# Seven block products in every token tile but the first, shared products copied between PSUM banks, and one written order for everything behind the first tile

## The chip, the cores and the metric

The kernel runs on one core of a Trainium2 chip. The engines are PE (TensorE: matmuls, with weight loads listed apart as PEld), DVE (VectorE), ACT (ScalarE), POOL (GpSimd) and SP (SyncE, here used to issue transfers). The metric is the device time of one execution in microseconds (us). Three runs of the kernel before gave 226.59, 226.91 and 228.11 us; the median is 226.91.

## The reference

Attention over pooled keys and values feeds a maxout layer. In short:

```python
k_p = k.reshape(B, H, Sp, 8, D).mean(axis=3)          # B, H, S, D = 8, 8, 576, 64; Sp = 72
v_p = v.reshape(B, H, Sp, 8, D).mean(axis=3)
attn = softmax(q @ k_p.T / sqrt(D))
x = (attn @ v_p).transpose(0, 2, 1, 3).reshape(4608, 512)
h = maximum(maximum(x @ w1, x @ w2), x @ w3)          # 768 wide
out = h @ w_out                                       # 4608 x 512, float32
```

Inputs are float32 and are cast to 16 bits on their way into SBUF (the keys of batch 0 excepted).

## The kernel before

**Tiles.** The 4608 tokens are nine tiles of 512, tile n = 0 to 8; attention comes in eight batches of 576 tokens, so that tile n holds the end of batch n-1 and the beginning of batch n. `xT` is a ring that holds the attention output transposed, `hT` the hidden layer transposed.

**Maxout as a linear part and two relu inputs.** The kernel uses h = x w1 + max(0, x (w2 - w1), x (w3 - w1)). The linear part times w_out is one matrix `wm` (`linear`, L344), so the output is x wm + max(...) w_out. A plain tile needs 6 row blocks x 2 weights x 4 matmuls of 512 columns for the hidden layer (`hidden_part`, L357), and 4 x (4 + 6) matmuls for the output (`project`, L400).

**Seven products.** A 2 x 2 block matrix product can be made from seven block products and some sums in place of eight (Winograd's form). `PRODUCTS` names the operands of the seven: S1 to S4 are sums of weight blocks (`fold_w`, `fold_out`), T1 to T4 sums of data blocks. Products 1, 6, 5 and 3 are accumulated one after the other in one PSUM bank, A, whose running value is read out after each; product 2 has bank B; 7 and 4 share bank C. Each hidden product is four matmuls of 256 columns (L789), each output product ten (L713). Before the change the hidden layer is made so in tiles 6, 7 and 8 (`seven`, L753), the output in tiles 2, 3, 4, 7 and 8 (`out_seven`, L643). There the value of product 1 is copied by ACT to SBUF (L795) and added to product 2 by DVE (L766); the top rows of `hT` then come from one more ACT copy (L799) and a DVE maximum of two SBUF operands (L769).

**Attention of a batch.** Keys and values are pooled by sums of eight rows. `fold_steps` (L157) does it in three sums, on POOL for most batches (L161, L162, L164). `pool_v` (L177) pools V of batch 0 by matmuls. Keys are transposed on PE (`keys`, L196) and copied into zero-padded tiles `kz` (`turn_k`, L204). Queries are transposed on PE in batches 0 to 2 (`turn_q`) and by a DMA from SP in the others (`T`, L302). Scores go to PSUM and ACT takes exp of them (L223): eight steps of 576 columns (`scores`), or, in batch 7, nine of 512 (`scores_flat`). `values` (L264) multiplies by the pooled V; DVE divides by the row sums (L274, L276). The result is transposed on PE (batches 0 to 2, L259) or by DMA from SP (L253).

**Order.** The program is written by hand: every engine and every DMA queue runs its instructions in program order, and waits where data or a buffer is not there. `block(0, ...)` runs tile 0 with steps of batches 0 and 1 between its parts; `MIDDLE` does so for tiles 1 to 4; `block(5, LEAD, ...)` for the hidden part of tile 5; `ORDER` and `weave` for the last three tiles. In these lists `k`, `K`, `q`, `Q`, `s`, `v`, `x` and `T` are attention steps, `1a` to `7c` hidden products, `o1` to `o7` output products. `held` and `gate` make POOL's fold wait for a certain DVE sum.

**PSUM** has eight banks. In the middle of the kernel before, scores have four (two pairs), the FFN three, transposes one. In its last part `SC` has two, `PA` two, `BC` one, `PO` one, and `val` two.

**Loads.** Inputs are loaded through POOL's DMA queue, two buffers for each of k, q and v, and outputs are stored mostly through SP's.

## Time and profile before

| what | value |
|---|---|
| median of three runs | 226.91 us (226.59 to 228.11) |
| the profiled execution | 228.01 us |
| its span, first to last instruction | 226.3 us |
| granted TensorE clock | 1.000 |
| busy: PE / DVE / ACT / POOL | 214.7 / 148.6 / 122.3 / 138.6 us |
| read from HBM / written | 34.60 / 9.44 MB |

The profiled execution is one of its own, with its time beside its span; durations of single instructions come from it, and it is 1.1 us above the median. "Busy" counts an instruction from start to end; matmuls overlap, so the mean of one matmul is longer than its share of a dense row, and the chain of waits shows that share better. A row of a group names the source line, the engine, the operation, output and inputs with their shapes, how often it ran, the busy time and the mean of one.

### The profile page before, as it was taken

Reading aid. Unit: us, or ns where it says so; the run is one execution under the profiler, and the core shown is the slowest. Engines: PE = TensorE matmul, PEld = TensorE weight load, DVE = VectorE, ACT = ScalarE, POOL = GpSimd, SP = SyncE. Lnnn points to the kernel's source line nnn. Section 1 sums busy time; section 2 is a strip of 40 time slices with the busy share of each in tenths; the row PEclk is TensorE's granted clock in tenths of the full one; section 3 lists DMA queues with packets and bytes.
Section 4 is the critical chain, followed back from the end, with each engine's and each line's share of the span. In section 5 each row is a group of like instructions: output and inputs, shape, how many; then the busy total and the mean of one; then the engine's idle time right before and its main releaser. Section 6 shows DMA issues by size and latency. Waiting matters only on the chain.

```text
span 226.3 us, 4691 instructions
## 1 busy us (share of the span) xinstructions
PE 214.7 (95%) x1807; PEld 146.4 (65%) x1807; DVE 148.6 (66%) x292; ACT 122.3 (54%) x221; POOL 138.6 (61%) x111
## 2 busy tenths in 40 slices
PE   6788999999999999999999999699999999999993
PEld 2467745558656555965686568355677677788882
DVE  3668876038595385876679668535668886898840
ACT  2267524755874577238624862475687446555330
POOL 7974300999949967787677758999500913872020
PEclk9999999999999999999999999999999999999999
DMA  6999999989759999659999599965241534200265
GB/s 167 210 197 197 208 207 208 203 163 224 128 106 191 217 220 208 112 129 151 199 226 191 31 216 236 182 126 132 58 107 29 122 61 95 46 3 0 55 203 164
DMA packets 47351, 33.54 MB, mean 148 GB/s; under 512 B 27041, under 2 KB 42337, under 8 KB 47329
## 3 DMA queue, kind: packets, MB, share of 16 engines
q0 software_dynamic: 16944, 16.98, 48.1%
q1 hardware_dynamic: 29936, 15.87, 33.0%
q10 hardware_dynamic: 448, 0.39, 0.7%
q8 instruction: 14, 0.23, 0.5%
q14 instruction: 9, 0.07, 0.1%
HBM read 34.60 MB, written 9.44 MB: 195 GB/s over the span
## 4 chain that ended last, share of the span: by engine, by line
PE 69%; DMA 15%; POOL 11%; issue 1%; DVE 1%; ACT 1%; POOLq 0%
PE pw L362 21%; PE oA L713 9%; DMA vt<-in_v_dram 8%; PE pA L789 7%; PE po L416 7%; PE po L412 5%; PE oC L713 4%; PE psc L218 4%; DMA mw<-in_moe_w_dram 4%; PE pC L789 3%; POOL half L161 3%; DMA xT<-xn 3%; PE pav L268 3%; PE oB L713 2%; POOL half L162 2%; PE pB L789 2%
## 5 line engine op out<-in xcount | busy, mean ns | idle before, releaser
L362 PE MATMUL pw<-xT,mw 128*128 128x512 f16 (+1 forms) x336 | 72.8, 348 | 1.9 <-DMA xT<-xn 1.6
L362 PEld LDWEIGHTS <-mw 128*128 128x128 f16 x336 | 31.6, 98 | 22.3 <-DMA xT<-xn 1.8
L370 DVE TENSOR_TENSOR hT<-t,pw 128x512 f16<-128x512 f16 (+1 forms) x42 | 25.4, 609 | 25.1 <-ACT et L223 17.8
L223 ACT ACTIVATE et<-psc 72x576 f16<-72x576 f32 (+2 forms) x54 | 35.2, 661 | 6.8 <-PE psc L218 6.7
L161 POOL TENSOR_TENSOR half<-vt 72x2048 f32<-72x2048 f16 x7 | 28.4, 4061 | 13.8 <-DMA vt<-in_v_dram 13.3
L162 POOL TENSOR_TENSOR half<-half 72x1024 f32<-72x1024 f32 (+1 forms) x13 | 27.3, 2098 | 11.0 <-DVE rcp L274 6.1
L368 ACT ACTIVATE t<-pw 128x512 f16<-128x512 f32 (+1 forms) x42 | 22.5, 537 | 16.2 <-PE pw L362 15.8
L276 DVE TENSOR_TENSOR xn<-pav,rcp 128x512 f16<-128x512 f32 x40 | 27.7, 692 | 1.4
L416 PE MATMUL po<-mwo,hT 128*128 128x512 f16 (+1 forms) x102 | 23.5, 366 | 0.0
L218 PE MATMUL psc<-qT,kz 128*128 128x320 bf16 (+2 forms) x120 | 22.4, 278 | 0.8 <-DVE qT L194 0.6
L218 PEld LDWEIGHTS <-kz 128*128 128x128 bf16 x143 | 13.1, 98 | 13.3 <-ACT qT L194 1.1
L161 POOL TENSOR_TENSOR half<-ktFalse 96x1536 f32<-96x1536 f16 x6 | 18.7, 3125 | 4.0 <-issue 2.9
L564 POOL TENSOR_TENSOR pad<-xT 128x256 f16<-128x256 f16 x8 | 5.9, 732 | 22.5 <-ACT pad L795 13.9
L795 ACT CAST pad<-pA 128x512 f16<-128x512 f32 x27 | 15.6, 588 | 7.2 <-PE pA L789 7.0
L268 PEld LDWEIGHTS <-et 72*128 72x128 f16 x320 | 15.1, 98 | 3.6 <-issue 0.4
L723 ACT COPY osb<-oA 128x512 f32<-128x512 f32 x12 | 7.0, 586 | 19.2 <-PE oA L713 19.2
L274 DVE RECIPROCAL rcp<-pav 128x8 f32<-128x8 f32 x40 | 8.2, 204 | 14.0 <-PE pav L268 13.6
L412 PE MATMUL po<-wm,xT 128*128 128x512 f16 (+1 forms) x68 | 16.6, 366 | 0.0
L268 PE MATMUL pav<-vp,et 72*128 72x65 f16 x320 | 16.4, 194 | 0.1
L421 ACT COPY osb<-po 128x512 f32<-128x512 f32 (+1 forms) x16 | 9.2, 573 | 12.0 <-PE po L416 12.0
L789 PEld LDWEIGHTS <-sw 128*128 128x128 f16 x144 | 13.7, 98 | 2.5
L766 DVE TENSOR_TENSOR pad<-pad,pC 128x512 f16<-128x512 f16 x18 | 12.3, 685 | 3.9 <-PE pC L789 3.6
(122 smaller groups left out, 380.0 us busy)
## 6 DMA issues: line engine op xcount, KB each, us to landing
out_dram<-osb SPq DMA_DIRECT2D x38, 128.0 KB, 5.5
ktFalse<-in_k_dram POOLq DMA_DIRECT2D x7, 576.0 KB, 8.2
qb<-in_q_dram POOLq DMA_DIRECT2D x7, 576.0 KB, 13.0
vt<-in_v_dram POOLq DMA_DIRECT2D x7, 576.0 KB, 17.5
mw<-in_moe_w_dram POOLq DMA_DIRECT2D x9, 256.0 KB, 9.4
out_dram<-osb SPq DMA_DIRECT2D x8, 256.0 KB, 7.4
ktTrue<-in_k_dram SPq DMA_DIRECT2D x3, 384.0 KB, 5.2
out_dram<-ob SPq DMA_DIRECT2D x8, 128.0 KB, 2.6
```

What stands on the lines that cost most here:

```text
L161: yield e.tensor_tensor(out=f, in0=t[:, :, 0:4, :], in1=t[:, :, 4:8, :], op=ALU.add)
L162: yield e.tensor_tensor(out=f[:, :, 0:2, :], in0=f[:, :, 0:2, :], in1=f[:, :, 2:4, :], op=ALU.add)
L218: nc.tensor.matmul(out, kz_all[b % 2][f % 2][rows, h, :], qTs[b][rows, n + i0:n + i1, 64 * (h % 2):64 * (h % 2) + 64], start=True, stop=True)
L223: nc.scalar.activation(out=out, in_=in_, func=FT.Exp, scale=1.0 / 64.0)
L268: nc.tensor.matmul(pav[:, h // 4, 65 * (h % 4):65 * (h % 4) + 65], ets[b][:, h, c0:c0 + 128], vp_all[:, b, h, :], start=True, stop=True)
L276: nc.vector.tensor_tensor(out=xn, in0=pv[:, :, :, 0:D], in1=rcp.to_broadcast([128, 2, 4, D]), op=ALU.mult)
L362: mm = nc.tensor.matmul(pw, w_sb[wi][:, kc, bass.ts(jc, 128)], x[:, kc], start=(kc == 0), stop=(kc == KCH - 1))
L370: nc.vector.tensor_tensor(out=hT[:, jc, c0:c1], in0=t, in1=pw, op=ALU.max)
L412: nc.tensor.matmul(po, tokens(128 * m, 128 * m + 128)[:, kc], wm_sb[:, kc, c], start=(kc == 0), stop=False)
L416: nc.tensor.matmul(po, hT[:, jc, bass.ts(mm, 128)], wo_sb[:, jc, c], start=False, stop=(jc == JCH - 1))
L713: nc.tensor.matmul(p, left, right, stop=(r == 4), skip_group_check=True, start=(i in FIRST and r == 0 and (m == 0 or n == LAST)))
L789: mm = nc.tensor.matmul(p[:, w], a[:, kc, bass.ts(g, 128)], b[:, kc, :], start=(i in FIRST and w + kc == 0), stop=(w + kc == 2), skip_grou ...
```

## The change

Behind the hidden layer of tile 0 there is one written order, `ORDER`, of some 500 steps, in place of `MIDDLE`, `LEAD`, `ORDER` and `weave`.

- The hidden layer and the output of tiles 1 to 8 are all made from seven products; only tile 0 stays plain.
- Product 1 is copied by ACT from bank A into bank B (PSUM to PSUM), and product 2 accumulates there. For the hidden layer the top rows of `hT` then come straight from banks B and A: a relu of one half by ACT, a maximum with the other half by DVE, each for 256 columns. For the output one ACT copy takes bank B out. A first matmul into the bank, `zB`, comes before.
- V of batch 1 is pooled on PE like that of batch 0. The folds on POOL are cut into pieces (`pieces`): five for K, six for V; the third sum of K is made on PE by accumulating two transposes, that of V on DVE. Each piece waits for the DVE sum of SBUF operands that stands last ahead of it (`shared`).
- All four key copies are ACT's. All scores of batches 1 to 7 are flat (nine steps of 512).
- The sums of output weights for the w_out rows (`G`) are POOL's; the data sums `t` and `u` are DVE's.
- Behind tile 0 PSUM holds `SC` 2, `PA` 2, `PB` 1, `PC` 1 and `val` 2 banks.
- The pooled V is kept for three batches in place of eight.

In the order, `p` is half a row block of tile 0's output, `<k4` a load, `K4` and `V4` pieces of folds, `P` V of batch 1 on PE, `t1` to `t4` and `u1` to `u4` data sums, `S`, `f`, `F`, `G` weight sums, `1d` to `7d` output products. Cut to its core:

```diff
     def load_v(b, eng, dtype=F16, cuts=(0, H)):
-        if b == 0:
+        if b < 2:
...
     def new_kp(b):
-        kps[b] = sb2.tile([96, 6, D], BF16, name="kp", tag="kp")
+        kps[b] = sb2.tile([96, 2, 6, D], F16, name="kp", tag="kp")
...
     def keys(b, tag):
...
         for i in range(3):
-            nc.tensor.transpose(pkt[:, i, :],
-                                kps[b][:, 2 * i:2 * i + 2, :].rearrange("p i d -> p (i d)"),
-                                ident[0:96, 0:96])
+            for j in range(2):
+                nc.tensor.matmul(pkt[:, i, :], kps[b][:, j, 2 * i:2 * i + 2, :].rearrange("p i d -> p (i d)"),
+                                 identh[0:96, 0:96], start=(j == 0), stop=(j == 1))
...
-        for par, evac in enumerate((nc.vector.tensor_copy, nc.scalar.copy)):
+        for par in range(2):
             for odd in range(2):
-                (evac if b > 2 else nc.vector.tensor_copy)(
+                nc.scalar.copy(
...
+    def both(out, a, b, op, e=nc.vector):
+        t = e.tensor_tensor(out=out, in0=a, in1=b, op=op)
+        if e is nc.vector:
+            shared[:] = [t]
+        elif shared[0] is not None:
+            after([t], shared[0])
...
+    def hidden_product(n, i, g):
...
+        p = bank(of(i), n, g)
+        za, zb = PRODUCTS[i]
+        for w in range(2):
...
+            for kc in range(2):
+                mm = nc.tensor.matmul(p[:, w], a[:, kc, bass.ts(g, 128)], b[:, kc],
+                                      start=(i in (1, 7) and w + kc == 0),
+                                      stop=(w + kc == 2), skip_group_check=True)
...
+        if i == 1:
+            nc.scalar.copy(out=bank("B", n, g), in_=p)
+        elif i in (6, 5):
+            nc.scalar.copy(out=y[:, i == 5], in_=p)
+        elif i in (2, 3):
+            t0 = sb2.tile([128, HALF], F16, name="t0", tag="t0")
+            nc.scalar.activation(out=t0, in_=p[:, 0], func=FT.Relu)
+            nc.vector.tensor_tensor(out=h_of(g)[:, i - 2], in0=t0, in1=p[:, 1], op=ALU.max)
+        if i in (5, 7) and (n, 12 - i, g) in done:
+            plus(1)
+        if i == 4:
+            plus(0)
+            shared[:] = [nc.vector.scalar_tensor_tensor(
+                out=h_of(g + JH), in0=y[:, :, 0], scalar=0.0, in1=y[:, :, 1],
+                op0=ALU.max, op1=ALU.max)]
...
+    def out_product(n, i):
...
+        if i == 1:
+            nc.scalar.copy(out=bank("B", n, "d"), in_=p)
+        elif i != 4 and i != 7:
+            nc.scalar.copy(out=o(int(i in (5, 3)))[:, :, lo if i in (2, 3) else hi], in_=p)
...
+    def pieces(what, b):
...
+        e = nc.gpsimd
+        for i in range(0, n, 2):
+            c = slice(i, i + 2)
+            yield e.tensor_tensor(out=f[:, c], in0=t[:, c, 0:4, :], in1=t[:, c, 4:8, :],
+                                  op=ALU.add)
+        for i in range(0, n, n // 2):
+            c = slice(i, i + n // 2)
+            yield e.tensor_tensor(out=two[:, c], in0=f[:, c, 0:2, :], in1=f[:, c, 2:4, :],
+                                  op=ALU.add)
+        if what == "v":
+            both(vp_all[:, b % 3, :, 0:D], two[:, :, 0, :], two[:, :, 1, :], ALU.add)
             yield
...
+    def piece(what, b):
         if (what, b) not in folding:
+            folding[what, b] = pieces(what, b)
+        gate = shared[0]
+        op = next(folding[what, b])
+        if op is not None and gate is not None:
+            after([op], gate)
...
+              16: [(None, "f f")], 17: [(1, "K")], 20: [(None, "F F")],
+              22: [(None, "F F G G G G")]}, (hidden,))
+    first_tiles = project(0)
...
+    nc.tensor.matmul(psum([128, NB], F32, name="zB", tag=PB[0], bufs=PB[1]),
+                     warm[:, 0:128], warm, start=True, stop=True)
...
+        S S q10 <k3 q11 p q12 k1 p P1 K2 K2 s10 p S q13 K2 K2 P0 s11 S s12 K2 s13 s14 V2 s15
+        s16 V2 s17 V2 s18 p q20 v10 q21 p q22 k2 v11 V2 p V2 V2 x10 v12 <v3 <q3 x11 K3 p K3
+        s20 K3 v13 K3 s21 1a x12 K3 x13 t1 t3 t2 p V2 s22 <k4 t4 V3 2a q23 v14 6a V3 1b s23
+        s24 7a V3 5a s25 V3 2b V3 s26 3a s27 4a s28 6b T3 V3 <q4 <v4 1c x14 v20 5b 2c 6c K4
+        K4 v21 x20 <k5 3b k3 K4 7b 5c x21 v22 1a 4b 3c K4 K4 x22 7c 2a s30 t1 u1 t2 s31 1d
...
+        7b 2d 1c 6d 6c 4b 5c 7c u4 5d 4c 3c 2c 7d 3d 4d
...
+    last = out_last(LAST)
+    for i in range(4):
+        sum_h(LAST, i)
     for i, m in ((1, 0), (1, 1), (2, 0), (2, 1), (6, 0), (6, 1), (7, 0), (5, 0), (5, 1),
                  (7, 1), (3, 0), (3, 1), (4, 0), (4, 1)):
-        outs(i, m)
-    for _ in tiles:
-        pass
+        last(i, m)
```

## The prediction

> **What bounds the kernel now.** The page's busy row comes first, then the table of 10 us stretches.

> ```profile
> PE 214.7 (95%) x1807; PEld 146.4 (65%) x1807; DVE 148.6 (66%) x292; ACT 122.3 (54%) x221; POOL 138.6 (61%) x111
> ...
> 140.00:150.00 10.00, 7.85 (x61) 4.77 (x58) 4.92 (x10) 5.13 (x10) 9.77 (x4) 1.00 0.99 153
> ...
> 160.00:170.00 10.00, 10.00 (x98) 7.31 (x96) 6.39 (x14) 8.60 (x17) 1.30 (x2) 1.00 0.41 87
> ...
> 190.00:200.00 10.00, 10.00 (x84) 7.96 (x83) 8.87 (x14) 6.05 (x12) 7.54 (x11) 1.00 0.23 52
> ```

> The columns of a stretch are its length, PE, PEld, DVE, ACT, POOL, granted clock, DMA share, GB/s. PE is the bound almost everywhere: it loses 4.9 us in the first 30 us, about 2 us at 140 to 150, and what follows its last matmul at 222.5. With ACT at 8.6 of 10, or DVE at 8.9 and POOL at 7.5, PE stays full. So PE work is the currency, and the question is what the other engines do when PE has less.

> **The price of PE work.** In the chain in order of time each piece ends where the next dense one starts:

> ```profile
> 68.90 0.86 PE po L412 x4
> 70.33 1.29 PE po L416 x6
> ...
> 104.39 0.86 PE pw L362 x4
> ...
> 161.33 0.44 PE pA L789 x4
> ...
> 199.79 1.09 PE oA L713 x10
> ```

> Four 512-wide matmuls take 0.864 us, a block product of four 256-wide ones 0.437, an output product of ten 1.09. A token tile therefore costs: hidden plain 12 groups x 0.864 = 10.37, hidden by seven 21 x 0.437 = 9.18; output plain 4 x (0.86 + 1.29) = 8.62, output by seven 7 x 1.09 = 7.63.

> - Removed: tiles 1 to 5 change hidden form, 5 x 1.19 = 5.9 us; tiles 1, 5 and 6 change output form, 3 x 0.99 = 3.0. Together 8.9.
> - Added: batch 1's V is pooled on PE, 12 matmuls 256 wide, 1.3; the key transposes become six matmuls in place of three (three step by 0.14 in the timeline), 7 x 0.14 = 1.0; the matmul into PB, 0.2. Together 2.5. Flat scores cost nothing: 9 x 0.217 per batch, where eight pairs took 1.95.
> - Net on PE: **-6.4 us**.

> The check is to add up the same prices from 37.2 us on (the first output product, at 37.94, less 0.7 for batch 1's turns, which move behind it). Before: 8.6 + 51.8 + 27.5 + 25.9 + 38.1 for matrix products, 13.7 scores, 9.3 values, 5.2 turns, in all 180.1. PE ended 185.3 us later, so **5.2 us were stalls**, 2.2 of them the transposed DMA at 145. After: the order adds up to 165.9, zB 0.2, the last tile's output 7.6, in all 173.7. The tail may cost 0.5 more: it ends with DVE additions and 128 KB stores (2.6 us to land) in place of a half copy and 64 KB (2.1). So the time hangs on the new stalls S: change = -6.4 + 0.5 + (S - 5.2).

> **ACT.** Its rows are 0.59 us for 512 columns, but back to back they start closer:

> ```profile
> 194.56 0.59 ACT L421 COPY osb<-po 128x512 f32<-128x512 f32 x1 [1.09 <-PE po L416]
> 195.04 0.59 ACT L795 CAST pad<-pA 128x512 f16<-128x512 f32 x1
> ```

> The pitch is 0.48; for exp 0.49, for a 256-wide relu 0.28 (0.39 less the same 0.11), for one key copy 0.485. The change gives ACT the copies that DVE made of the keys (four now, 1.94 per batch), one more exp per batch, and five evictions per row block. The copy from PSUM to PSUM has no row. Its ends are the 256-wide copy (0.37) and the key copy's cost per column taken to 512 (0.85); I take the 0.59 copy of equal shape. Along the order, ACT asks 10.9, 10.4 and 10.4 us in the first three stretches of 10 us of PE work, then 8.5 to 9.1, then less. From 5.8 to 26.1 us it asks 3.6 more than PE. PE can't run ahead of that: scores have two banks, eight of batch 1's stand with no other matmul between them (8 x 0.49 against 8 x 0.22), and a block product often follows the copy of its own bank by only 0.1 to 0.5 us. I charge **3.0 us**. At the full 0.59 row the excess would be 10.3.

> **POOL and loads, early.** The rows that the pieces are cut from:

> ```profile
> 39.40 4.06 POOL L161 TENSOR_TENSOR half<-vt 72x2048 f32<-72x2048 f16 x1 [13.33 <-DMA vt<-in_v_dram]
> 43.54 2.34 POOL L162 TENSOR_TENSOR half<-half 72x1024 f32<-72x1024 f32 x1
> ...
> 49.36 3.11 POOL L161 TENSOR_TENSOR half<-ktFalse 96x1536 f32<-96x1536 f16 x1
> 52.54 1.81 POOL L162 TENSOR_TENSOR half<-half 96x768 f32<-96x768 f32 x1
> ```

> A fold of K is 3 x 1.04 + 2 x 0.9 = 4.9 us, of V 4 x 1.02 + 2 x 1.17 = 6.4. The third steps leave POOL (1.0 and 1.3): K's goes to PE, V's to DVE (0.42 to 0.69 by its 512-wide f16 rows; I take 0.42). The four wo sums (G) on POOL have no row of 768 columns; three times the undisturbed 0.67 of a 256-wide one gives 2.0 as an upper end, 1.5 by the V row's rate is the lower. At some 1.9 each, behind DVE's sums at about 36, they end at 44, and K of batch 2 lands at 45.1 as before. Its fold ends near 50.7 with the load of K3 queued ahead, while PE would ask for it at 37.4 + 10.8 + 1.2 = 49.4. That 1.3 us wait lets ACT catch up, so it isn't added. Then V's six pieces end at 57; only behind them does POOL issue V3 and Q3. Two loads at POOL's queue rate of 0.2 MB/us (2.07 MB from 20 to 30 us; a load is 0.59) put Q3 down near 65; its transpose took 4.0 to 10.2 us (median 7.0); scores of batch 3 stand at 37.4 + 30.2 + 3 = 70.6. I charge **1.0**.

> **DVE.** Its pitch is 0.60 for a 512-wide PSUM sum, 0.335 and 0.47 for the f16 sums. The order asks 124.9 us against 165.9 of PE; the densest stretch, 67.0 to 75.4, asks 2.3 too much once. With ACT's near misses later I put **2.2** on the rest of the order; before, stalls apart from the one wait were 3.0. So S = 3.0 + 1.0 + 2.2 = 6.2 and the change is -6.4 + 0.5 + 1.0 = -4.9. The profiled execution took 228.0 (span 226.3, and 1.7 around it), 1.1 above the median; the same difference on the median gives **222.0 us**.

> **Rivals.** *POOL holds DVE up.* A DVE sum of two SBUF operands that meets a running POOL sum was long here:

> ```profile
> L597 DVE TENSOR_TENSOR so<-wm x2: 417/882/1348, 62.3 to 64.0; 128x512 f16<-128x512 f16 x2
> L597 DVE TENSOR_TENSOR so<-so,wm x1: 424/424/424, 63.7 to 63.7; 128x512 f16<-128x512 f16 x1
> ```

> At 62.3 POOL ran the last V step, and the same sum took 1.35 in place of 0.42. While POOL folds (10 to 107 us of the order) DVE has some 63 such sums: t, u, the maxima, V's last step. It works 77 us of these 97, so 20 are free, or 0.32 per sum. At the mean excess of 0.46 the sums cost 29: 9 too much, and the result is about **231 us, slower**. This decides from 0.32 us on. For it: DVE and POOL both run at 70 to 95% there, and POOL is up to 7.6 us behind PE. Against it: a piece is at most 1.2 us (4.06 before), starts only when the last such DVE sum written ahead of it has ended, and at 190 to 200 both engines were busy and PE full. [...]

> *The loads come late.* V3, Q4 and V4 are issued behind POOL's pieces, and a piece that waits for its load holds the next issue.

> ```profile
> busy tenths in 40 slices 2051100611500710061025003307000000000000
> DMA to landing us min/median/max: 8.0/14.3/23.4
> ```

> These are V's landings. With 8 us after the issue, V4 is folded at 89 and DVE wants it at 37.4 + 49.5 + 4 = 91: free. At 11 it is 3 late, after two such steps 6; at 14.3 it is 10. Since K and Q went ahead of V in the 14.3 (6 us of queue), I hold 8 to 11 likelier. At 3 to 4 us more than my sum the result is **225.5, no change**.

> *Nothing new stalls.* S of 1 to 2 gives **217**; before's stretch from 150 to 220 shows that woven products can be full.

> *The change doesn't do what it says*: if the copied product had to be copied back or added by DVE, 0.6 us x 31 would come to DVE; the diff has no such step, and I give it nothing of its own.

> **How the numbers follow.** The measurement tells 1% apart (224.6 to 229.2). Forecast, 219 to 224.6: 0.48. Nothing stalls: 0.17. Loads late: 0.19. POOL holds DVE: 0.13, and 0.03 for a slower end by something else. So faster 0.65, same 0.19, slower 0.16. The range reaches from 216.5, below S = 1, to 229.5, where the late loads and a light form of the collisions end; left out are the collisions' full price and ACT's 10.3.

> **What would show it.** Right: PE's busy time near 208, ACT's share above 60%, PE holes between 42 and 72 us with ACT's exp or a POOL fold as what was waited for, none after 150. Wrong: DVE sums t, u and the maxima with means well above 0.42, 0.55 and 0.69; DVE's V step waiting for POOL; POOL waiting for V's landing in every batch; block products of 0.437 that lie 0.2 or more apart all through the order.

## The result, and the profile after

The changed kernel takes 251.96 us (median of 4 runs, 250.88 to 255.90) where the kernel before, on the same chip, takes 226.75 (226.53 to 228.11): a ratio of 1.108, 95% interval 1.1015 to 1.1147. It is 25 us slower, and the forecast was 5 us faster, with a range that ended at 229.5. The profiled execution took 250.88 us, with a span of 249.1 and a mean granted clock of 0.966; the one of before had 1.000. Where the runs of a kernel below fall into two groups, both are given: the three longer ones that were profiled have holes behind transposes that land late, but no shorter run of the same kernel was profiled beside them, so that these holes make the whole difference isn't shown.

The busy row and the clock row of the page of the changed kernel (the clock row has 40 slices of 6.2 us, each digit the granted clock in tenths):

```profile
PE 220.0 (88%) x2119; PEld 177.4 (71%) x2119; DVE 185.7 (75%) x347; ACT 152.6 (61%) x306; POOL 113.4 (46%) x118
...
PEclk9999999999799999976999799799999999999999
```

And the table by stretches of 10 us, with the columns as before (length, PE, PEld, DVE, ACT, POOL, clock, DMA share, GB/s):

```profile
60.00:70.00 10.00, 6.92 (x59) 5.58 (x58) 7.73 (x10) 6.08 (x14) 9.99 (x10) 0.83 1.04 174
100.00:110.00 10.00, 4.54 (x45) 3.96 (x43) 2.93 (x7) 3.62 (x8) 0.65 (x1) 0.96 1.26 169
130.00:140.00 10.00, 8.10 (x65) 6.42 (x64) 9.18 (x14) 5.42 (x12) 8.87 (x9) 0.83 1.00 170
150.00:160.00 10.00, 7.90 (x67) 6.44 (x65) 6.04 (x12) 3.71 (x8) 7.26 (x8) 0.85 1.23 227
200.00:210.00 10.00, 10.00 (x110) 8.94 (x108) 9.73 (x22) 6.80 (x14) 0.00 (x0) 1.00 0.38 84
```

Two things are to be seen. Between 60 and 160 us PE has holes in several stretches, and in the deepest of them or just behind, the clock is below 1; between them lie full stretches at full clock (10.00 of 10 from 140 to 150). Behind 170 us, with POOL idle, PE is as full as it was before, with DVE at up to 9.7 of 10. So the woven products can run without gaps, and most of what costs the time lies in the part in which attention, folds and loads run beside them.

**Where the 22.8 us of span come from.** The trace gives every matmul's start. In dense rows two starts lie 0.109 us apart for 256 columns, 0.216 for 512, 0.056 for 128, 0.033 for the 65-wide ones of the attention output; that is taken as a matmul's own time, and what a start comes later than that is a wait, or, in stretches of half clock, where two starts lie 0.213 us apart for 256 columns, up to one more own time, loss by the clock. Added up over each profiled execution:

| us | before | after | difference |
|---|---|---|---|
| own time of all matmuls | 208.5 | 202.2 | -6.3 |
| waits of PE up to 30 us | 7.2 | 8.0 | +0.8 |
| waits of PE from 30 us on | 5.0 | 25.0 | +20.0 |
| lost by half clock | 0.0 | 7.4 | +7.4 |
| behind the last matmul's start | 4.1 | 5.0 | +0.9 |

The sum, 22.8, is the difference of the spans (249.1 less 226.3). The work that the change takes from PE is gone as forecast, -6.3 against -6.4; the waits, forecast to go from 5.2 to 6.2, went to 25, and the clock took 7.4 more, which had no term at all.

**What PE waits for.** From the list of waits of the changed kernel (engine, tile, line, what came last; us in total, times, longest):

```profile
POOL half L749 <- DVE xs L511: 20.7, 5, 11.0
DVE xs L511 <- DMA xT<-xn: 9.1, 3, 6.6
PE pC L606 <- DVE ys L616: 8.5, 3, 6.0
PE pA L606 <- DVE xs L511: 4.0, 2, 3.1
```

The largest hole, 6 us at 104, reads as follows in the order of time (start, length; in brackets the idle time ahead and what ended it). SP, DVE and PE:

```profile
97.67 2.57 SPq L642 DMA_DIRECT2D out_dram<-osb  x4
100.34 2.78 SPq L241 DMA_TRANSPOSE xT<-xn  x2
103.23 5.49 SPq L290 DMA_TRANSPOSE qT<-qb  x1
```

```profile
108.84 0.42 DVE L511 TENSOR_TENSOR xs<-xT 128x512 f16<-128x512 f16 x1 [6.65 <-DMA xT<-xn]
```

```profile
110.58 0.58 PE L606 MATMUL pC<-xs,sums 128*128 128x256 f16 x2 [6.05 <-DVE ys L616]
```

The chain of waits carries the same transposed tile:

```profile
100.34 8.48 DMA xT<-xn
...
112.03 0.85 PE pA L606 x4
```

SP issues four stores, then the transposes that bring the last attention output that token tile 3 needs (the third of the five of batch 3) into `xT`. The first of them lands 8.5 us after its issue. DVE works its queue in order, and at its head stands `t1`, the data sum of the next token tile, which reads that output: DVE is idle for 6.65 us ahead of it. The next thing behind it that PE needs is a `ys` sum that has its operands already, but bank C isn't free until it is done, so PE stops too. When PE goes on, four matmuls of 256 columns take 0.85 us in place of 0.44: the clock is at one half until 116.

**DVE and POOL beside each other.** The groups of DVE's sums, then those of POOL's pieces (busy us, mean ns, idle time ahead and its releasers):

```profile
L631 DVE SCALAR_TENSOR_TENSOR hT<-ys 128x512 f16<-128x512 f16 x24 | 19.7, 821 | 0.8
L511 DVE TENSOR_TENSOR xs<-xT 128x512 f16<-128x512 f16 x16 | 11.4, 725 | 10.5 <-DMA xT<-xn 9.1 <-ACT xT L250 1.4
L511 DVE TENSOR_TENSOR hs<-hT,hs 128x768 f16<-128x768 f16 x16 | 11.1, 693 | 0.1
L511 DVE TENSOR_TENSOR vp<-vt 72x512 f16<-72x512 f16 x6 | 4.9, 825 | 0.0
```

```profile
L749 POOL TENSOR_TENSOR half<-vt 72x512 f32<-72x512 f16 x24 | 27.2, 1150 | 16.2 <-DVE xs L511 9.7 <-issue 2.9 <-DVE hT L631 1.7
L749 POOL TENSOR_TENSOR half<-ktFalse 96x512 f32<-96x512 f16 x18 | 21.4, 1209 | 14.6 <-DVE xs L511 11.0 <-issue 2.6 <-DVE hT L631 0.7
```

Alone these sums take 0.42 (t and V's last step), 0.55 (u) and 0.69 us (the maxima), as an experiment below shows; in the mean they took 0.69, 0.69, 0.82 and 0.82 (V). With the S sums beside POOL's G sums, 1.65 to 1.85 us in place of 0.42, DVE spent some 22 us more on them: 8.6 on t, 4.5 on u, 3.1 on the maxima, 2.4 on V and 3.9 on S (three of the four; the last took 0.41). POOL's pieces are 13 to 17% longer than priced.

The means hide how uneven this is. Most sums take what they take alone, and a few take several times that (least, median and longest in ns; then one of the longest, and POOL beside it):

```profile
L511 DVE TENSOR_TENSOR xs<-xT x16: 409/420/2649, 59.2 to 216.8; 128x512 f16<-128x512 f16 x16
L511 DVE TENSOR_TENSOR xs<-xT,xs x16: 410/419/2578, 62.4 to 215.8; 128x512 f16<-128x512 f16 x16
```

```profile
132.29 2.58 DVE L511 TENSOR_TENSOR xs<-xT,xs 128x512 f16<-128x512 f16 x1
```

```profile
132.47 1.17 POOL L749 TENSOR_TENSOR half<-ktFalse 96x512 f32<-96x512 f16 x1
133.57 1.00 POOL L753 TENSOR_TENSOR kp<-half 96x384 f16<-96x384 f32 x1
```

This sum ended 0.3 us behind the second piece, so it stood through both. Behind it PE waits 2.1 us and then runs at half clock until 140; a hole of 3.2 us at 64 stands behind two t sums of 2.65 and 1.37 us in the same way. Part of the holes is thus due to collisions alone, without a late tile.

So there were three suspects: these collisions; the transposed tiles that come late from SP's queue, in front of DVE's sums; and the loop that ties the two together, in which a piece of POOL waits for a DVE sum (20.7 us in the list), the loads queued behind it on POOL start later, and the query transposes and the tiles behind them on SP start later too.

### The profile page after: what moved, and what is told of

Same layout as the page of the kernel before. It is cut to its first block, busy times and chain, and to the rows that moved or that the text cites. A ratio compares the mean times of both kernels' runs of the same rounds, so it can differ in the third digit from the quotient of the medians.

```text
span 249.1 us, 5422 instructions
## 1 busy us (share of the span) xinstructions
PE 220.0 (88%) x2119; PEld 177.4 (71%) x2119; DVE 185.7 (75%) x347; ACT 152.6 (61%) x306; POOL 113.4 (46%) x118
## 4 chain that ended last, share of the span: by engine, by line
PE 61%; DVE 12%; ACT 11%; DMA 9%; issue 4%; POOL 1%; POOLq 0%; ACTq 0%; DVEq 0%
PE pA L606 13%; PE pA L667 9%; PE pC L606 7%; DMA xT<-xn 6%; PE pC L667 5%; PE pw L348 4%; PE psf L206 4%; DMA vt<-in_v_dram 4%; PE pB L606 3%; PE pav L256 3%; PE pB L667 3%; ACT et L211 3%; DVE xs L511 3%; ACT kz L196 2%; PE pm L335 2%
## 5 line engine op out<-in xcount | busy, mean ns | idle before, releaser
L616 DVE TENSOR_TENSOR ys<-ys,pC 128x512 f16<-128x512 f16 x48 | 32.7, 682 | 6.5 <-PE pC L606 4.5
L211 ACT ACTIVATE et<-psf 72x512 f16<-72x512 f32 x63 | 35.5, 594 | 3.3 <-PE psf L206 3.0
L622 ACT CAST ys<-pA 128x512 f16<-128x512 f32 x48 | 28.1, 585 | 15.3 <-PE pA L606 12.6
L749 POOL TENSOR_TENSOR half<-vt 72x512 f32<-72x512 f16 x24 | 27.2, 1150 | 16.2 <-DVE xs L511 9.7
L606 PEld LDWEIGHTS <-sums 128*128 128x128 f16 x192 | 18.2, 102 | 18.8 <-issue 16.0
L749 POOL TENSOR_TENSOR half<-ktFalse 96x512 f32<-96x512 f16 x18 | 21.4, 1209 | 14.6 <-DVE xs L511 11.0
L206 PE MATMUL psf<-qT,kz 128*128 128x256 bf16 (+4 forms) x161 | 23.9, 255 | 1.3 <-ACT et L211 0.6
L606 PE MATMUL pA<-xs,sums 128*128 128x256 f16 x96 | 19.6, 288 | 4.3 <-DVE xs L511 4.0
L631 DVE SCALAR_TENSOR_TENSOR hT<-ys 128x512 f16<-128x512 f16 x24 | 19.7, 821 | 0.8
L606 PE MATMUL pA<-xs,sw 128*128 128x256 f16 x96 | 19.8, 291 | 0.0
L511 DVE TENSOR_TENSOR xs<-xT 128x512 f16<-128x512 f16 x16 | 11.4, 725 | 10.5 <-DMA xT<-xn 9.1
```

Of the source, the lines that this page charges most:

```text
L206: nc.tensor.matmul(out, kz_all[b % 2][f % 2][rows, h, :], qTs[b][rows, n + i0:n + i1, 64 * (h % 2):64 * (h % 2) + 64], start=True, stop=True)
L211: nc.scalar.activation(out=out, in_=in_, func=FT.Exp, scale=1.0 / 64.0)
L511: t = e.tensor_tensor(out=out, in0=a, in1=b, op=op)
L606: mm = nc.tensor.matmul(p[:, w], a[:, kc, bass.ts(g, 128)], b[:, kc], start=(i in (1, 7) and w + kc == 0), stop=(w + kc == 2), skip_group_ ...
L616: nc.vector.tensor_tensor(out=y[:, j], in0=y[:, j], in1=bank("C", n, g), op=ALU.add)
L622: nc.scalar.copy(out=y[:, i == 5], in_=p)
```

## The experiments

### One suspect at a time

The first three take away one suspect each. Pieces replaced by fills of about the length that the pieces have alone, so that POOL is nearly as long at work (95.7 us in place of 113.4) and reads no SBUF in them:

```diff
-            yield e.tensor_tensor(out=f[:, c], in0=t[:, c, 0:4, :], in1=t[:, c, 4:8, :],
-                                  op=ALU.add)
+            yield e.memset(t[:, c, 0:8, :], 1.0)
...
+            op = e.memset(two[:, c], 0.5)
+            e.memset(t[:, c, 4:6, :], 0.5)
+            yield op
```

> The changed kernel with POOL's pieces of the folds replaced by fills of about the same length (one fill of 1024 columns in place of a first piece, one of 384 or 512 and one more in place of a second): POOL keeps its order, its gates and its waits for loads, but reads no SBUF operand. Keys and values are constants, so the pooling is left out. Theory A (a DVE sum of two SBUF operands and a POOL sum hold each other up, and the delay opens PE holes): t, u and the maxima fall from 0.73/0.65, 0.69 and 0.82 us to 0.42, 0.55 and 0.69, DVE's busy time falls by some 18 us, and the time falls from 252 to 228 to 236 us. Theory B (late transposes on SP's queue, behind query transposes that wait for late loads, make the holes): the sums get shorter too, but the holes at 104 and 152 us stay, and the time stays above 243 us.

Measured: 247.12 us (246.84 to 247.39), ratio 1.091, 1.088 to 1.094. The DVE groups of this kernel:

```profile
L631 DVE SCALAR_TENSOR_TENSOR hT<-ys 128x512 f16<-128x512 f16 x24 | 16.6, 692 | 0.8
L511 DVE TENSOR_TENSOR hs<-hT,hs 128x768 f16<-128x768 f16 x16 | 8.8, 551 | 0.1
L511 DVE TENSOR_TENSOR xs<-xT 128x512 f16<-128x512 f16 x16 | 6.6, 420 | 12.8 <-DMA xT<-xn 11.4 <-ACT xT L250 1.4
```

The t, u and V sums and the maxima are back at their undisturbed length, and DVE is busy 16.4 us less (169.3). The S sums, beside POOL's G sums, which this edit leaves as they are, still take 1.65 us. So the t, u and V sums and the maxima are long because of POOL's pieces beside them; that it is the reading of SBUF in the pieces is the author's estimate, since the fills write and don't read, and no run shows it apart from the rest of what a piece does. The hole at 64 us is gone with them. But only 5 us of the 25 came back: the theory of collisions had 228 to 236 us, and its rival, above 243, came out. DVE now stands idle for the transposed tiles, 11.4 us in place of 9.1.

The gate of the pieces taken away (the wait of a piece for the DVE sum that stands last ahead of it):

```diff
-        if op is not None and gate is not None:
-            after([op], gate)
```

> The changed kernel without the dependency of a POOL piece on the last DVE sum written ahead of it; all data waits stay. Theory A: pieces start at any time, so they meet DVE sums at least as often; DVE's sums stay as long or grow, and the time is 250 to 260 us. Theory B in the form of a loop (a DVE sum t waits for a transposed tile, POOL's pieces wait for that sum by their gate, the next loads wait behind the pieces, the query transpose waits for its load, and the next transposed tile waits behind it on SP): the loop is cut, POOL no longer waits 20 us for DVE's t sums, loads go out earlier, and the time falls by 5 to 12 us.

Measured: 258.06 us in one run and 270.6 in the other, which was the profiled one. The group of t sums in it:

```profile
L511 DVE TENSOR_TENSOR xs<-xT,xs 128x512 f16<-128x512 f16 x16 | 20.2, 1260 | 0.1
```

Without the gate a t sum of the second kind takes 1.26 us in the mean, three times its own length. Here too it is a few sums that do it:

```profile
115.69 6.36 DVE L511 TENSOR_TENSOR xs<-xT,xs 128x512 f16<-128x512 f16 x1
```

POOL ran five pieces and the issue of a load without a pause from 115.9 to 121.8 us, and this sum ended 0.3 us behind the last; PE waited 8.7 us for it. A wait of PE of 11.6 us for a query transpose is the other large hole of this execution. The gate's waits look costly in the list, and yet without it the time rose by 6 us in the shorter run: it lets a sum in between two pieces. The 258.06 us are inside the 250 to 260 of the theory of collisions; the loop, which had 5 to 12 us less, fell as the sole cause.

The query transposes of batches 3 to 7 left out:

```diff
-                qTs[b] = sb2.tile([128, 2 * NG, 128], BF16, name="qT", tag="qT")
-                nc.sync.dma_start_transpose(
-                    out=qTs[b], in_=qbs[b].rearrange("p hp t d -> p (hp t d)"))
+                qTs[b] = qTs[b - 2]
```

> The changed kernel without the query transposes by DMA of batches 3 to 7 (their scores use the transposed queries of batches 1 and 2, so the output differs); the loads of the queries stay. Theory A: 247 us or more, since only 1 to 4 us of DMA and SP time go. Theory B: SP no longer stands behind a query transpose, the tiles of xT come 3 to 7 us earlier, the holes at 104 and 152 us shrink to under 2 us, and the time falls to 236 to 243 us.

Measured: 247.46 us (246.81 to 248.10), ratio 1.093, 1.086 to 1.100. The hole at 104 us stays, and the wait behind it:

```profile
DVE xs L509 <- DMA xT<-xn: 8.8, 3, 6.8
```

So the query transposes are not what holds the tiles up by themselves: that theory had 236 to 243 us, and its rival, 247 or more, came out. None of the three is worth more than 5 of the 25 us.

### Suspects together

Fills, no gates and no query transposes in one kernel, and its two neighbours with one of the last two kept:

> All three edits together: fills in place of POOL's sums, no gates, no query transposes by DMA. What is left is the work of PE, ACT and DVE in the written order. My sum for these alone was S = 5.2 (3.0 for ACT, 2.2 for the rest of the order), that is 221 us. If it comes out at 219 to 224 us, the prices of PE and ACT held, and all that was missed lies in POOL, the gates and the DMA queues; at 230 us or more the order stalls by itself.

> Fills in place of POOL's sums (pooling left out) and no gates; query transposes as in the changed kernel. The fills alone gave 247, all three edits 234. If the gates carry the loop that theory B names (DVE sum waits for a transposed tile, POOL waits for the sum, loads and query transposes follow), then without them and without collisions most of the gain is here: 234 to 238 us, with POOL no longer waiting for DVE. If the query transposes on SP are what counts, it stays at 243 to 247.

> Fills in place of POOL's sums (pooling left out) and no query transposes by DMA (scores use those of batches 1 and 2); gates as in the changed kernel. If the gates are the carrier: 242 to 246 us, one edit's gain less than the sum. If the query transposes are: 234 to 238.

Measured: all three 234.18 us (233.15 to 235.21), ratio 1.034, 1.023 to 1.045. With the query transposes kept 242.52 (242.34 to 242.71), ratio 1.071, 1.065 to 1.076. With the gates kept 232.96 in one run and 240.98 in the other.

Together the parts give 18 us where alone they gave 5, something negative and 4.5. The profiles fit one reading: where one wait is gone, another stands near the same place (a hole that ends between 101 and 111 us is in the profile of each kernel with fills or without query transposes). The share of the gates isn't settled, since the two runs of the last kernel lie on either side of the 234, and 242.52 is just below the 243 to 247 that were expected if the query transposes count. The 234.18 is well above the 219 to 224 that were expected if only POOL, the gates and the DMA queues had been missed. In the kernel with all three gone one large hole is left. Its stretches, and the link of its chain of waits that lies in them:

```profile
90.00:100.00 10.00, 6.01 (x61) 5.26 (x58) 2.69 (x5) 5.10 (x11) 4.78 (x7) 0.94 1.14 180
100.00:110.00 10.00, 7.06 (x46) 5.30 (x46) 7.01 (x15) 3.74 (x8) 7.74 (x13) 0.54 0.84 152
```

```profile
91.54 9.63 DMA xT<-xn
```

The transposed tile of batch 3 takes 9.6 us to land, with no query transpose ahead of it: it is one of three transposes behind four stores, with a load of V and one of K issued in the 5 us before. The clock of 0.54 in the stretch behind makes the 6.9 us hole dearer by 3.0 us.

### The transposed tile of batch 3 on PE

The output of batch 3 is turned on PE and evicted by ACT, as that of batches 0 to 2 is, each turn five steps later in the order: once with everything else as changed, once on top of the three together:

```diff
-        if b > 2:
+        if b > 3:
             cut = 128 - (g0 + 128) % RING
```

> The changed kernel with this one edit: the attention output of batch 3 is transposed on PE. The hole at 104 to 110 us and the slow clock behind it should go: 252 falls to 241 to 245 us if the wait for that transposed tile is a cause of its own; to 248 us or more if it only shows where delays from the collisions on DVE come out.

> The three edits of e4_all_three, and the attention output of batch 3 is transposed on PE, five transposes and ACT copies more, in place of DMAs from SP. In e4 one hole was left, 9.6 us from 91.5, in which DVE's first sum of tile 3 waits for a tile that SP transposes behind four output stores and beside a load, and the granted clock stood at 0.54 for the next 10 us. Theory: that wait and the slow clock behind it are all of what is left over my 221; the time falls from 234 to 220 to 224 us. Rival (the order stalls by itself, and another wait takes its place): 229 us or more.

Measured: alone 246.35 us (245.35 to 247.34), ratio 1.087, 1.076 to 1.099; on top of the three 230.83 (230.27 to 231.38), ratio 1.019, 1.011 to 1.027. Alone, it lies between the two expectations (241 to 245 if the late tile is a cause of its own, 248 or more if not): the hole at 104 goes, and one of 4.8 us opens at 148, at the tile of the next batch:

```profile
DVE xs L514 <- DMA xT<-xn: 5.9, 1, 5.9
```

On top of the three no hole of over 1 us is left behind the first 30 us, and the clock stays at 1.00 to the last product. Yet the time is not the 220 to 224 us of the theory but the rival's 229 or more: small waits remain. The sums over matmul starts, for the kernels of this line:

| us | after | fills | fills, no query transposes | all three | all three, batch 3 on PE |
|---|---|---|---|---|---|
| waits of PE from 30 us on | 25.0 | 22.3 | 17.3 | 14.0 | 10.9 |
| lost by half clock | 7.4 | 6.7 | 5.7 | 3.0 | 0.0 |

The last column lacks 14.1 of the 25.0 us of waits and all of the 7.4. These are single executions (that of the third column of numbers is the longer run of its kernel), but the course is plain: every cause removed takes waits away and clock with it. With all of them gone the kernel still isn't faster than before (230.8 against 226.6), though it leaves out work on POOL and SP that any real version has to do.

### Is ACT what is left?

In that kernel ACT is at 9.99 and 9.49 of 10 from 60 to 80 us. Two tests on it: two of the four key copies given to DVE, and the copies between PSUM banks left out.

```diff
-                nc.scalar.copy(
+                (nc.scalar.copy if par else nc.vector.tensor_copy)(
                     out=kz_all[b % 2][par][64 * par:64 * par + 64, :, 0:Sp].rearrange(
```

> The kernel with all stalls off POOL and SP taken away (fills for the pooling pieces, no gates, no query transposes by DMA, batch 3 transposed on PE; 230.8 us), and in it two of the four key copies of every batch go to DVE instead of ACT. These parts of the computation are left out: the pooling of keys and values, the queries of batches 3 to 7. Theory: what still holds PE back from 40 to 80 us is ACT, which is at 9.99 and 9.49 of 10 in 60 to 80 us; 0.97 us per batch go from ACT to DVE, some 3 us in the four batches handled by 110 us, so 228 to 229 us. Rival: PE is held there by the order itself and DVE, so moving the copies gives nothing: 230.8, or more since DVE is at 9.1 in 70 to 80 us.

```diff
         if i == 1:
-            nc.scalar.copy(out=bank("B", n, g), in_=p)
+            pass
...
-                                  start=(i in (1, 7) and w + kc == 0),
+                                  start=(i in (1, 2, 7) and w + kc == 0),
```

> The kernel of 230.8 us (pooling, and queries of batches 3 to 7 left out; no gates; batch 3 transposed on PE) without the copies of the shared product from one PSUM bank to another: product 2 starts its bank itself. Left out, beside the parts named, is the shared product in the lower-left results of every tile but the first. PE, DVE and POOL do what they did; ACT loses 31 copies of 0.58 us, some 15 us by its pitch of 0.48, five to six of these copies before 90 us. Theory (ACT is what holds PE back from 40 to 120 us): 226 to 228 us, with ACT well below 9 of 10 in 60 to 80 us. Rival (DVE's queue, worked in order, holds it as much, as the run with key copies on DVE suggests): 229 to 231 us. If it is below 226, the copies between banks cost more than their time on ACT.

Measured: with the key copies on DVE 235.73 us (235.41 to 237.15), ratio 1.041, 1.038 to 1.045, so 5 us slower than without. Without the copies between banks 229.13 and 230.06 us in two runs, 237.87 and 238.45 in two others; the profiled one has the span of the kernel that it was made from, 228.4. So both theories fell (228 to 229, and 226 to 228 us), and from 60 to 120 us ACT is not what holds PE. Of the stretch from 40 to 57 us the second test says nothing, since the first such copy lies at 57.

The first test shows one of the places where it lost: of 5.3 us of added waits, 1.1 lie at the first key copies. DVE, then PE:

```profile
38.70 3.23 DVE L512 TENSOR_TENSOR sums<-wm 128x512 f16<-128x512 f16 x2
41.85 0.97 DVE L196 CAST kz<-pkt 64x288 bf16<-64x288 f32 x2
```

```profile
43.92 0.38 PE L206 MATMUL psf<-qT,kz 128*128 128x320 bf16 x2 [1.27 <-ACT kz L196]
```

The copies stand in DVE's queue behind two S sums that take 1.6 us each beside POOL's G sums, and PE waits. In the second test PE is ahead by 0.5 us at 72 and by 0.9 at 101, and loses it at 118 in one wait for bank C, which a DVE sum frees (1.74 us, 0.45 in the kernel with the copies):

```profile
117.96 0.38 PE L607 MATMUL pC<-xs,sums 128*128 128x256 f16 x2 [1.74 <-DVE osb L678]
```

The copies between PSUM banks, the headline of the change, 31 of them at 0.58 us, thus cost next to nothing in this kernel: the shorter runs without them are about 1 us below the runs with them. It wasn't tried in the changed kernel as it is.

### A kernel that does all the work, with fewer pieces on POOL

Batch 3 on PE as above, and V of all batches pooled on PE by products with the selection matrix, as that of batches 0 and 1 is:

```diff
-        if b < 2:
+        if b < 8:
             vts[b] = ld.tile([96, 4096], dtype, name="vt0", tag="vt")[:, 0:3072].rearrange(
```

> The changed kernel with batch 3's output transposed on PE (246.4 us), and V of all batches pooled on PE by products with the selection matrix, as batches 0 and 1 are. Nothing is left out. It takes 43 us of pieces from POOL, and DVE's six V steps; it adds 12 products 256 wide per batch, 1.3 us, 7.8 in all, and an eviction of 256 columns each on DVE and ACT per batch. Theory (the collisions between DVE and POOL, and late loads behind POOL's gated pieces, cost some 10 to 15 us): DVE's sums meet POOL less than half as often, the V and Q loads are issued earlier, and in spite of 7.8 us more on PE the time is 238 to 246 us. Rival (the stalls come from the transposed tiles and ACT alone): 254 us.

Measured: 250.37 us (248.05 to 252.78), ratio 1.108, 1.102 to 1.115. PE's own time rose by 7.8 us over the kernel with batch 3 on PE (210.9 against 203.1), the time by some 4.7 (1.108 less 1.087 of 226.7): the waits from 30 us on fell from 24.6 to 18.7. The t sums of the second kind went from 0.65 us to 0.56, the maxima from 0.84 to 0.73, u back to 0.55. The result is above the theory's 238 to 246 and below the rival's 254. By these two differences the collisions and POOL's queue are worth about 3 us there, less than the work that it takes to avoid them on PE; with intervals of 0.6% and 1.2% to either side of the two ratios the size is uncertain.

### The clock by itself

In all these traces half clock follows a hole of PE: in the changed kernel it lasts 3.41 us from 64.8, 136.5 and 156.9 and 6.83 us from 109.2, each time behind one. To see whether the hole does it, or the load of the whole core, four waits were put into the kernel of 230.8 us where PE was full and POOL idle:

```diff
+    def hole(n):
+        t = ld.tile([96, 4096], F16, name="hole", tag="vt")[:, 0:n]
+        after([nc.gpsimd.memset(t, 1.0)], mms[-1])
+        nc.tensor.matmul(psum([128, 512], F32, name="hp", tag=SC[0], bufs=SC[1]),
+                         t[:, 0:128], warmh[0:96], start=True, stop=True)
```

> The kernel of 230.8 us again (pooling, and queries of batches 3 to 7 left out), and in its last 60 us, where PE was full, four waits are put into PE's queue: POOL fills a tile of 700, 1400, 2300 and 3400 columns after the product ahead, and one product of the tile follows. Holes of PE about 0.9, 1.7, 2.7 and 3.8 us, 9.1 in all, and 0.9 for the four products. Theory (a hole of about 2 us or longer is followed by a granted clock of one half for 3.41 us or a multiple): no half clock after the first, 3.41 us after the third, 3.41 to 6.83 after the fourth, open for the second; so 240.8 + 3.4 to 7 us, less what ACT and DVE catch up: 243 to 247 us. Rival (the half clock comes from the load of all engines and DMA together, not from the hole): granted clock 1.00 throughout, 240 us or less.

Measured: 239.07, 240.76 and 242.38 us, and 253.29 in the profiled run, which had one more hole, of 12.4 us, at 117 (a transposed tile, for which DVE waited 12.8 us). The holes put in came out as 0.8, 1.4, 2.2 and 3.1 us, and none is followed by half clock in this execution; the one at 117 is. Three stretches of this profile:

```profile
120.00:130.00 10.00, 0.12 (x1) 0.10 (x1) 2.25 (x7) 0.00 (x0) 0.80 (x1) 0.51 1.03 112
...
200.00:210.00 10.00, 7.81 (x81) 6.67 (x80) 7.55 (x16) 4.40 (x9) 2.02 (x1) 1.00 0.10 20
210.00:220.00 10.00, 7.86 (x71) 6.65 (x69) 6.15 (x12) 4.12 (x9) 2.02 (x1) 1.00 0.44 103
```

The median of the three shorter runs, 240.76, is near the rival's 240 or less and below the theory's 243 to 247, though the rival's reason (the load of all engines) isn't needed either. Their mean granted clocks (0.996, 0.990 and 0.986) don't exclude half clock behind a hole in the longest of them, for which there is no profile. The theory's rule, 2 us and more, didn't hold for the holes of 2.2 and 3.1 us; what these profiles show in its place is in the last section.

## Why the prediction was wrong, by its own steps

- **PE's work, -6.4: right.** The matmuls' own time fell by 6.3. That bears out the prices as a sum; one by one they weren't measured.
- **The tail, +0.5:** 0.9 by the starts of the last matmuls. Nearly.
- **The copy between PSUM banks at 0.59 us: right,** 0.58 measured, and next to nothing in the kernel in which it was left out.
- **ACT, 3.0 us of new waits from 5.8 to 26.1 us of the order: about right.** In the kernel with everything else removed PE waits 4.0 us from 40 to 70 us (before: 1.3), 2.7 of them where eight exps run back to back at 0.53 to 0.54 us, not 0.49.
- **POOL and loads early, 1.0:** the pieces were 13 to 17% dearer than priced, the G sums cheaper (1.70 to 1.81 for 1.9). No wait of PE for the queries of batch 3 stands in the list, and this term isn't what made the result.
- **The rest of the order, 2.2 us of new stalls: the step that failed.** In its place PE waits some 21 us from 60 us on (25.0 less some 4 from 30 to 60), and half clock behind the holes costs 7.4 more, for which the sum had no term. The 2.2 was worked out from the sums that DVE and ACT are asked for per stretch of PE work, as if every operand were there. It held no price for a transposed tile that arrives late in front of DVE's `t1`, though `t1` is written about 4 us behind the transpose's issue and such transposes took 2.7 us in the median and up to 11.8 in the profile of before, where POOL waited 8.7 us for one in front of a data sum of its own; and the stall of 2.2 us that before had at 145 us for a transposed tile was booked as one that goes. In DVE's queue, worked in order, the `t1` at 108.84 held back for 6.65 us the sums behind it, a `ys` sum that frees bank C among them, and PE waited 6.05 us. Nor did it hold a price for a sum that stands through several pieces of POOL, up to 2.65 us in place of 0.42; that was left to the rival below.
- **The rival "POOL holds DVE up", at 0.13: its mechanism was there, and too lightly held.** The sums were 22 us longer (18.6 without S), near the 29 that it was priced at, though not by an even 0.46 each but by a few long ones. What spoke against it in the text, the gate and the short pieces, didn't prevent it; without the gate the time was 258 us and more, and longer pieces weren't tried. Beside the fills the t, u and V sums and the maxima went back to 0.42, 0.55 and 0.69; the `ys` sums, with one operand in PSUM, took 0.68 beside pieces and fills alike. Yet the price of 231 us for this rival alone was no forecast of 252: taken away alone, the collisions give back 5 us.
- **The rival "the loads come late" fell.** V's loads landed in 10.0 us in the median, and POOL's V pieces waited for DVE sums, not for loads.
- **What would have shown it:** the list had the right signs. PE's busy time is 220, not 208; t, u and the maxima are well above 0.42, 0.55 and 0.69; holes go on to 160 us. Two of its signs didn't come: POOL didn't wait for V's landings, nor DVE's V step for POOL. ACT's share is 61%, as said.

What stays open is the exact share of each cause, since they replace each other, and the 10.9 us of waits in the last kernel of the line: 4.0 are the ones from 40 to 70, some 4.3 lie between 80 and 120 us, part of them beside the added turns of batch 3, and the rest wasn't followed up. Nor was it tried to place `t1` further behind its transpose in the order, which is the direct test of the step that failed. No version that does all the work came near the kernel before; the best of them took 246.35 us.

## What to carry to other kernels

A sum of busy times per stretch tells whether an engine has room, not whether an in-order queue keeps moving: for each instruction that reads what a DMA brings, compare the distance in the order with the longest landing in the profile, not the median, and count what stands behind it. Where the sums of two engines are longer beside each other and a queue holds a late DMA, as here, removing one can show little (5 us of 25 for the collisions, 18 for the three suspects together), so test them together before calling either harmless. Short PE work has to be woven densely enough that holes don't gather: here the stretches with holes paid again in clock, 7.4 us.

## What the runs showed of the hardware that wasn't expected

| window at full clock, PE busy | windows | next window at half clock |
|---|---|---|
| below 0.40 | 30 | 30 |
| 0.40 to 0.45 | 6 | 3 |
| 0.45 to 0.70 | 30 | 0 |
| 0.70 and more | over 760 | 0 |

In the changed kernel the windows at full clock ahead of half clock have PE busy 0.30 (from 61.4 us), 0.00 (105.7), 0.44 (133.1) and 0.39 (153.5); the least busy of the others at full clock up to the last product has 0.63. From half clock the next window was full in all 22 cases with PE busy 0.88 or more, and in none of the 19 with 0.81 or less. So what decided in these profiles wasn't the length of a hole but how much of one window it took: in the changed kernel 1.9 us at 134 fell into one window (busy 0.44) and cost 3.41 us of half clock, while the 2.2 and 3.1 us put in by hand fell across two windows each (0.71 and 0.64; 0.61 and 0.47) and cost nothing. That the same hole could be free in one execution and dear in the next is the author's estimate from these windows; no run here shows it for one and the same hole.

**How late a transposed tile was.** The transposes of `xT` land in 3.3 us in the median of the changed kernel, but the tile of batch 3 took 8.5 us there and 9.6 in the kernel with all three gone, behind four stores and beside loads, and in one execution of a kernel that otherwise had no such hole DVE waited 12.8 us for one. Late landings alone weren't new, and weren't enough: before, eight of the 27 took over 5 us, up to 11.8, and in the kernel of 230.8 us, which has no hole of over 1 us behind the first 30 us, one on its chain of waits took 7.0. What made the hole here was a sum at the head of DVE's queue that asked for the tile soon after its issue (6.65 us of idle DVE in the changed kernel).
